# Instruction order of five engines from a list scheduler, other loads and masks for the first blocks, and a finer first FFN group, in a fused attention and FFN kernel

## The chip, the core and the metric

The kernel runs on one core of one Trainium2 chip. The metric is the device time of one execution in microseconds (us). Ratios between kernels are the mean time of one kernel's fast runs over the mean time of the other's fast runs of the same rounds on the same chip, so they are not quite the ratios of the medians that are quoted beside them.

## The reference

Sliding-window attention with four sink keys, then an RMS norm and a gated FFN. Batch, heads, sequence and head size are 4, 8, 768 and 64; the window is 128; the FFN takes 3072 tokens from 512 to 1536 and back.

```python
# (cut and condensed: scale, pos and rel are as usual)
def _attn_ref(q, k, v, n_sink, window):
    scores = scale * np.matmul(q, k.transpose(0, 1, 3, 2))
    keep = (pos[None, :] < n_sink) | ((rel >= 0) & (rel < window))
    scores = np.where(keep, scores, -1e9)
    a = np.exp(scores - np.max(scores, axis=-1, keepdims=True))
    a = a / (np.sum(a, axis=-1, keepdims=True) + 1e-09)
    return np.matmul(a, v)

def _moe_ref(x, w_gate, w_val, w_out, rms_g):
    xn = x / np.sqrt(np.mean(x * x, axis=-1, keepdims=True) + 1e-06) * rms_g
    g = xn @ w_gate
    return (g * (1.0 / (1.0 + np.exp(-g))) * (xn @ w_val)) @ w_out
```

The 3072 tokens are 24 blocks of 128, six blocks to a batch. Four blocks form an FFN group, so there are six groups, 0 to 5.

## The kernel before

A block goes through these steps: load q, k, v (the software DMA queue casts fp32 to bf16); transpose q and k (on PE up to block 11, by DMA from block 12 on); scores on PE; exp on ACT; mask on DVE (on POOL from block 12, but for the first block of a batch); AV on PE; normalise on DVE; square on ACT; six small RMS steps and the scaling `xr` on DVE; transpose `xr`; then the FFN of its group. Once in a batch the first four keys are copied into a sink tile, `ksk`, on DVE.

```python
    X_DMA_FROM = 8
    QK_DMA_FROM = 12                       # q, k of later blocks are transposed by DMA
    MANUAL = {mybir.EngineType.PE, mybir.EngineType.SP}
    # ... pools ...
    ring = ctx.enter_context(               # 8 PSUM banks, used in turn
        tc.tile_pool(name="ring", bufs=8, space=bass.MemoryType.PSUM))
    # ...
    load_q(0); load_k(0); load_q(1); load_v(0)   # (cut) all on the software queue
    # ...
    def unit_sink(b):
        ks = sink.tile([P, HP * KSW], BF16, name="ksk")
        nc.vector.memset(ks, 0.0)
        # ...
            nc.vector.tensor_copy(          # reads the transposed k of the batch's first block
                out=ksv[pr, :, hi * NS:(hi + 1) * NS], in_=QKT[b][pr, 1, :, 0:NS])
    # ...
        def gate():
            st["pg"] = slot("pg")
            mms(st["pg"], wg, G, fts, cols)
            # ... th = tanh(pg / 2) on ACT
        def val():
            pvl = slot("pvl")
            mms(pvl, wv, G, fts, cols)
            # ... p1 = (th + 1) * pg ; hT = p1 * pvl, both on DVE; they free the banks
    # ...
    with tc.manual_schedule(engines=MANUAL):
        # units of attention are woven by hand between the parts of the FFN
        for ft in range(0, FTN, 2):        # group 0 in two halves of two blocks
            fa += parts_f(0, (ft, ft + 1), slice(0, GN // 2))
            fb += parts_f(0, (ft, ft + 1), slice(GN // 2, GN))
        # ...
```

`MANUAL` names the engines that follow the written order. DVE, ACT and POOL are not among them: the framework's own scheduler orders these.

The softmax here doesn't subtract the row's maximum and nothing guards it: scores larger than these inputs give would overflow.

## Time and profile before

| | before |
|---|---|
| median of 3 runs | 270.05 us (269.97 to 270.92) |
| span of the profiled run | 269.7 us, granted clock 0.994 |
| first scores / first FFN matmul (PE timeline) | 10.33 / 23.22 us |
| first gate matmul of group 1 | 91.57 us |
| last matmul of the last projection starts | 265.49 us |

The first gate matmul of group 1 is the useful place to cut the run in two. The prediction took it from the chain of waits, where the step begins at 91.74; the PE timeline has the instruction at 91.57. The two cuts differ by 0.17 us and nothing hangs on that.

The page's line of engines (busy us, share of the span, instructions), and after it the first line of its chain of work that ended last:

```profile
PE 240.3 (89%) x1698; PEld 128.5 (48%) x1698; DVE 179.0 (66%) x471; ACT 135.5 (50%) x267; POOL 96.9 (36%) x128
```

The chain, as shares of the span by engine:

```profile
PE 80%; DVE 7%; ACT 6%; DMA 4%; issue 1%; POOL 0%; ACTq 0%; POOLq 0%
```

The windows view gives the busy time of each engine in a stretch, the granted clock, a DMA share (not used here) and the GB/s moved. Cut at the two marks of the table:

```profile
core 0: us, PE busy (x) PEld busy (x) DVE busy (x) ACT busy (x) POOL busy (x), PEclk, DMA share, GB/s
0.00:91.57 91.57, 66.26 (x634) 46.01 (x635) 60.09 (x184) 53.49 (x104) 70.74 (x90) 0.98 1.99 157
91.57:265.49 173.92, 173.92 (x1066) 82.51 (x1063) 118.96 (x288) 81.41 (x163) 26.20 (x38) 1.00 0.35 65
265.49:269.70 4.21, 0.16 (x1) 0.00 (x0) 0.00 (x0) 0.60 (x1) 0.00 (x0) 1.00 0.16 62
```

The middle row is a wall: PE is busy in all of its 173.92 us. The top row is where time can be won: PE is idle there for 91.57 - 66.26 = 25.3 us. The view of waits says what PE stood for before group 1 (total, times, longest):

```profile
PE pT L303 <- ACT qkT L237: 6.7, 5, 4.2
PE pqk L218 <- DMA qs<-in_q_dram: 4.8, 1, 4.8
PE pv L361 <- DVE et L325: 3.1, 5, 0.9
PE pxt L423 <- DVE y L384: 2.7, 1, 2.7
PE pxt L423 <- DVE xr L404: 2.1, 2, 1.1
```

The longest of the first line, 4.2 us, has ACT as its releaser, but ACT is not its cause. The chain in order of time leads further back, to a DMA transpose of block 12, four blocks ahead of the work in hand:

```profile
70.07 0.53 ACT qkT L237
70.59 7.69 DMA qkT<-ks
...
80.69 0.91 ACT qkT L237
```

And the timeline of DVE, then that of PE, shows how it got into the chain (start, duration, line, operation; in brackets the wait ahead of it and what ended it):

```profile
78.31 0.35 DVE L256 COPY ksk<-qkT 64x16 bf16<-64x16 bf16 x2 [3.64 <-DMA qkT<-ks]
78.69 0.18 DVE L368 RECIPROCAL rden<-pv 128x4 f32<-128x4 f32 x1
```

```profile
81.64 0.61 PE L303 MATMUL pT<-qkT 64*128 64x256 bf16 x8 [4.23 <-ACT qkT L237]
```

The framework had put the sink copy of batch 2 early in DVE's order. DVE stood there for 3.64 us until the transpose landed. The normalising of two AV results, whose matmuls had ended by 75.3 us, lay behind it, then squares on ACT, then the copy that the next scores need. The Trainium skill, "TensorE: Matmul & The Clock Gate", Part 1 (in the note on the array's architecture), says that ACT and DVE queues are strictly first in, first out; this trace agrees, with 3.64 us spent in front of work whose inputs were there.

The same page says the array runs at half clock until some 3.4 us of sustained work and again after an idle window as long. This trace agrees on the half rate: eight 128x256 gate matmuls take 1.87 us at 23 us and 0.87 from 31 us on, and after the 4.23 us gap 512-column matmuls start 0.427 us apart, and 0.216 again from 86 us.

### The profile page before, as it was taken

The page shows a single profiled execution, that of the slowest core. Times are in us where ns is not written, and L with a number is a line of the kernel's source. Part 1 is how long each engine was busy: PE and PEld are TensorE (multiplying, and loading weights), DVE is VectorE, ACT ScalarE, POOL GpSimd, SP SyncE. Part 2 cuts the span into 40 slices and gives each one's busy share as a digit, 9 for nine tenths or more (in the row PEclk, how much of TensorE's full clock was granted, in tenths as well). Part 3 has the DMA queues.
Part 4 walks back from the last instruction along what each step waited for, and adds up shares of the span by engine and source line. Part 5 has one row for each costly group of instructions (what it writes and reads, how often), then busy time and mean ns, then how long its engine had stood idle before and what let it go on. Part 6 is the DMA issues. An engine that isn't in the chain of part 4 may idle for free.

```text
span 269.7 us, 4662 instructions
## 1 busy us (share of the span) xinstructions
PE 240.3 (89%) x1698; PEld 128.5 (48%) x1698; DVE 179.0 (66%) x471; ACT 135.5 (50%) x267; POOL 96.9 (36%) x128
## 2 busy tenths in 40 slices
PE   1746997997748899999999999999999999999993
PEld 0324685784425444444454444445444544444441
DVE  2573499798736699982699845998528893087700
ACT  2453576677726664555566445664554531333311
POOL 8987477489968510043043200412430100000000
PEclk9999999999997999999999999999999999999999
DMA  8999999999999999217322054121231111210022
GB/s 55 135 159 193 199 156 193 175 156 149 162 145 177 159 177 100 58 29 168 79 58 43 19 133 129 31 45 19 60 100 39 21 22 39 78 39 2 0 78 78
DMA packets 105912, 25.99 MB, mean 96 GB/s; under 512 B 97185, under 2 KB 102817, under 8 KB 105890
## 3 DMA queue, kind: packets, MB, share of 16 engines
q0 software_dynamic: 80672, 14.16, 70.2%
q1 hardware_dynamic: 25218, 11.54, 19.7%
q8 instruction: 13, 0.21, 0.3%
q14 instruction: 9, 0.07, 0.1%
HBM read 28.31 MB, written 6.29 MB: 128 GB/s over the span
## 4 chain that ended last, share of the span: by engine, by line
PE 80%; DVE 7%; ACT 6%; DMA 4%; issue 1%; POOL 0%; ACTq 0%; POOLq 0%
PE pg L438 22%; PE pvl L438 22%; PE po L482 21%; PE pT L303 5%; DMA qkT<-ks 3%; PE pv L361 2%; PE pqk L218 2%; DVE et L325 2%; ACT qkT L237 2%; DMA ks<-in_k_dram 2%; PE pv L356 2%; PE pv L345 1%; DVE x L369 1%; PE pss L279 1%; ACT et L312 1%
## 5 line engine op out<-in xcount | busy, mean ns | idle before, releaser
L438 PE MATMUL pg<-xnt,wg 128*128 128x512 bf16 (+1 forms) x336 | 74.9, 352 | 1.3 <-ACT xnt L427 1.3
L438 PE MATMUL pvl<-xnt,wv 128*128 128x512 bf16 (+1 forms) x336 | 74.9, 352 | 0.0
L451 ACT ACTIVATE th<-pg 128x512 bf16<-128x512 f32 x72 | 43.3, 601 | 54.5 <-PE pg L438 54.2
L459 DVE SCALAR_TENSOR_TENSOR p<-th,pg 128x512 bf16<-128x512 bf16 x72 | 49.1, 682 | 32.3 <-ACT th L451 31.8
L482 PE MATMUL po<-wo,hT 128*128 128x512 bf16 x288 | 67.0, 383 | 0.0
L312 ACT ACTIVATE et<-pT 128x512 bf16<-128x512 f32 (+1 forms) x96 | 46.4, 568 | 13.1 <-PE pT L303 13.0
L467 DVE TENSOR_TENSOR hT<-p,pvl 128x512 bf16<-128x512 bf16 x72 | 49.3, 685 | 3.4
L327 POOL TENSOR_SCALAR_AFFINE_SELECT et<-et 128x512 bf16<-128x512 bf16 x20 | 14.5, 730 | 91.4 <-ACT et L312 83.0
L438 PEld LDWEIGHTS <-wv 128*128 128x128 bf16 x336 | 32.4, 99 | 28.8 <-issue 1.0
L438 PEld LDWEIGHTS <-wg 128*128 128x128 bf16 x336 | 32.2, 99 | 29.2 <-issue 2.3
L482 PEld LDWEIGHTS <-hT 128*128 128x128 bf16 x288 | 27.2, 99 | 30.8 <-issue 2.0
L488 ACT ACTIVATE osb<-po 128x512 f32<-128x512 f32 x24 | 14.4, 601 | 30.9 <-PE po L482 26.9
L98 POOL DMA_DIRECT2D ks<-in_k_dram x24 | 21.3, 888 | 8.5 <-DMA wo<-in_moe_w_out_dram 2.9
L98 POOL DMA_DIRECT2D qs<-in_q_dram x24 | 21.5, 894 | 7.2 <-DMA wo<-in_moe_w_out_dram 2.1
L325 DVE TENSOR_TENSOR et<-et,masks 128x1024 bf16<-128x1024 bf16 (+1 forms) x28 | 18.0, 651 | 8.5 <-ACT et L312 8.3
L376 ACT ACTIVATE sq<-x 128x512 bf16<-128x512 bf16 x24 | 15.1, 628 | 16.4 <-DVE x L369 16.4
L303 PE MATMUL pT<-qkT 64*128 64x256 bf16 (+1 forms) x192 | 15.4, 279 | 8.5 <-ACT qkT L237 6.7
L111 POOL DMA_DIRECT2D v<-in_v_dram x24 | 21.3, 888 | 4.4 <-DMA qs<-in_q_dram 1.4
L369 DVE TENSOR_TENSOR x<-pv,rden 128x256 bf16<-128x256 f32 x48 | 19.8, 420 | 0.6
L361 PE MATMUL pv<-v,et 128*128 128x65 bf16 x192 | 17.3, 200 | 3.1 <-DVE et L325 3.1
L404 DVE SCALAR_TENSOR_TENSOR xr<-x,r,gb 128x512 bf16<-128x512 bf16 x24 | 19.1, 798 | 0.6
L303 PEld LDWEIGHTS <-qkT 64*128 64x128 bf16 x192 | 7.9, 96 | 17.9 <-issue 17.2
(57 smaller groups left out, 178.5 us busy)
## 6 DMA issues: line engine op xcount, KB each, us to landing
out_dram<-osb SPq DMA_DIRECT2D x24, 256.0 KB, 2.0
qs<-in_q_dram POOLq DMA_DIRECT2D x24, 128.0 KB, 7.6
ks<-in_k_dram POOLq DMA_DIRECT2D x24, 128.0 KB, 7.4
v<-in_v_dram POOLq DMA_DIRECT2D x24, 128.0 KB, 8.2
wg<-in_moe_w_gate_dram POOLq DMA_DIRECT2D x4, 384.0 KB, 9.9
wv<-in_moe_w_val_dram POOLq DMA_DIRECT2D x4, 384.0 KB, 10.5
wo<-in_moe_w_out_dram POOLq DMA_DIRECT2D x2, 768.0 KB, 10.4
xnt<-xr SPq DMA_TRANSPOSE x16, 2.5
```

The costliest lines, as they stand in the source:

```text
L98: nc.gpsimd.dma_start(out=tl, in_=src[b, :, t * P:(t + 1) * P, :].rearrange("h t d -> t h d"),)
L111: nc.gpsimd.dma_start(out=V16[b][:, t, :, 0:D], in_=v[b, :, t * P:(t + 1) * P, :].rearrange("h t d -> t h d"),)
L303: nc.tensor.matmul(out=pT[(u, hi)][:, j * 256:j * 256 + w], lhsT=QKT[b][pr, 1, hp, t * P:(t + 1) * P], rhs=QKT[b][pr, 0, hp, t * P:t * P + w],
L312: nc.scalar.activation(out=et[:, 2 * hi:2 * hi + 2, 0:nq, :].rearrange("p x n c -> p x (n c)"), in_=pT[(u, hi)].rearrange("p (j c) -> p j ...
L325: nc.vector.tensor_tensor(out=ev, in0=ev, in1=mv, op=ALU.mult)
L361: nc.tensor.matmul(out=dest, lhsT=E[(g, u)][:, x, 0, :], rhs=V16[b][:, t, h, :], start=(t == 0), stop=True, skip_group_check=True,)
L369: nc.vector.tensor_tensor(out=x16[:, 4 * u:4 * u + 4, :], in0=pvv[:, :, 0:D], in1=rden.unsqueeze(2).to_broadcast((P, 4, D)), op=ALU.mult,)
L438: nc.tensor.matmul(out=ps[:, i * n:(i + 1) * n], lhsT=w_sb[:, kt, ft * P:(ft + 1) * P], rhs=XNT[G][:, kt, cols], start=(kt == 0), stop=(kt ...
L451: nc.scalar.activation(out=st["th"], in_=st["pg"], func=ACT.Tanh, scale=0.5,)
L459: nc.vector.scalar_tensor_tensor(out=p1, in0=st["th"], scalar=1.0, in1=st["pg"], op0=ALU.add, op1=ALU.mult,)
L467: nc.vector.tensor_tensor(out=HT[key][:, i:i + n, cols], in0=p1.rearrange("p (n c) -> p n c", n=n), in1=pvl.rearrange("p (n c) -> p n c", ...
L482: nc.tensor.matmul(out=st["po"], lhsT=HT[(G, ft // 2)][:, ft % 2, tb * P:(tb + 1) * P], rhs=wo[:, ft, :], start=(ft == 0), stop=(ft == FTN ...
```

## The change

The intent: let a small list scheduler inside the kernel decide the order on all engines, instead of a hand-made weave on PE and SP and the framework's order on the rest; and make the first blocks come sooner.

1. Every step becomes an operation of a plan, with a duration, its needs, a priority and the PSUM banks it takes and frees. A simulation in the kernel takes, again and again, the operation that can start earliest. Its order is then issued as the written order of all engines. Each bank is assigned by the plan.
2. q and k of blocks 0 and 1 are loaded as fp32 by the hardware queues of SP and ACT and cast on DVE.
3. Masks of blocks 0 and 1 are added on PE: -30000 by a matmul into the score banks, four of 512 columns for each block.
4. FFN group 0 runs block by block (128-wide matmuls, four columns of tiles at a time).
5. The weights come in other chunks and earlier than block 4; some PSUM copies may go to DVE or ACT, as the plan finds best.

```diff
-    MANUAL = {mybir.EngineType.PE, mybir.EngineType.SP}
+class Plan:
+    HOP = {"PE": 40, "ACT": 35, "DVE": 35, "POOL": 90, "SP": 60}
+    def run(self):
+        while left:
+            for e, found in cand.items():
+                for o in found:                       # earliest start wins, then priority
+                    ready = o["ready"] + self.HOP[e] if o["ready"] else 0
+                    if k:                             # k PSUM banks needed
+                        ready = max(ready, sorted(self.banks.values())[k - 1] + 40)
+                    key = (max(free[e], ready), o["prio"], ready, o["at"])
 ... (cut)
+    F32_LOADS = 2
+    PE_MASKS = 2
 ... (cut)
+    for g in range(F32_LOADS):
+        sp(370, 1300, lambda g=g: load_f32("q", q, g, nc.sync), (), [("qst", g)], -90 + g, work=900)
+        op({"ACT": (100, 1300, lambda g=g: load_f32("k", k, g, nc.scalar))}, ...)
+        for n in "qk":
+            dve(335, lambda n=n, g=g: cast(n, g), [(n + "st", g)], [(n, g)], -9 + g)
 ... (cut)
+            pe((240, 480, 590)[min(t, 2)], lambda g=g, u=u: av(g, u), ...)
+            dve(430, lambda g=g, u=u: normal(g, u), ...)
+        dve(1650, lambda g=g: rms(g), ...)            # seven instructions, one operation
+                sp(1250, 1700, lambda n=n, g=g: dma_t(n, g), ...)   # DMA transposes of q, k
 ... (cut)
+            for tb in range(GB):                      # group 0, block by block
+                for i in range(FTN // 4):
+                    ffn(G, 3 * tb + i, range(4 * i, 4 * i + 4), slice(tb * P, (tb + 1) * P), ...)
 ... (cut)
-    with tc.manual_schedule(engines=MANUAL):
+    order = plan.run()
+    with tc.manual_schedule():
+        for *_, fn, o in order:
+            if fn is not None:
+                fn()
```

The numbers in the calls are the plan's durations in nanoseconds.

## The prediction

> **What bounds it now.** The chain of waits is 80% PE. From group 1's first gate matmul (91.74 us) to the last projection (265.67), the windows view shows PE busy 173.91 of 173.93 us: pure matmul at its fast rate (four 128x512 take 0.86 us). The tail (eviction, store) is 4.03 us. All slack lies in the first 91.74 us: PE busy 66.4, idle 25.3. That work at its later rate would take about 52 us, an estimate from durations in the trace: FFN group 0 20.8, its projection 10.4, scores and AV of blocks 0 to 8 9, transposes 7, the rest 4. So some 14 us of "busy" is slow clock: eight 128x256 gate matmuls take 1.87 us at 23 us, 0.87 later. The Trainium skill, "TensorE: Matmul & The Clock Gate", Part 1, says the array runs at half clock until about 3.4 us of sustained work, and again after an idle window as long; the trace agrees: after a 4.23 us gap ending at 81.64, AV matmuls take 0.06 us each instead of 0.03. That gap: DVE, in order, stood 3.64 us at a sink copy waiting for a DMA transpose that took 7.7 us beside saturated loads; AV, squares and the copy for the next scores lay behind it.
>
> **What the change does.** PE work stays nearly equal: group 0's columns in 128-wide instead of 256-wide matmuls, plus eight 128x512 mask matmuls (1.7 to 3.4 us, early, while PE has slack). DVE loses four masks (0.69 each), gains four casts (about 0.4) and some transpose copies from ACT. By group 1's start DVE still has about 60 us of work (60.3 before): FFN 16, RMS 14, normalising 10, masks 9, the rest copies, sinks, constants. So DVE, at 85 to 90% use, sets the length of the early stage afterwards, not PE.
>
> Hardware queues without issue on POOL (1.01 and 0.88 us each) bring the first scores from 10.3 to about 7 us and the first FFN matmul from 23.2 to about 16; group 0 begins with one block instead of two. Weights move ahead of block 4. The Trainium skill, "DMA: Bandwidth & Descriptors", "Issuing engines are not separate DMA queues", says other queues save only issue time, so supply does not grow: block 7 lands near 45 us, ahead of need. Ordering all engines by expected readiness removes most early stalls and the 4.2 us gap.
>
> **Sum.** First gate of group 1 at about 73 us instead of 91.7 (about 8 us from the first 31 us, 10 from the rest). After that PE stays dense: 174 us (DVE needs only 119 of it, ACT 81); tail 4. Predicted 251.5 us, 8 in 10 between 246.5 and 259. Chances: faster by over 2% 0.93, within 2% 0.06, slower 0.01.
>
> **What would show it.** Right: PE idle before group 1 under 18 us; DVE over 80% busy from 15 to 70 us; PE busy in total 225 to 233 (240.3 before); first group-1 gate to last projection within 2 us of 174; tail within 0.5 of 4.03. Wrong: PE idle of some us after group 1's start, led by "DVE hT" or DMA transposes.
>
> **What would make it wrong.** Fixed orders on strict queues: where planned durations are too low (0.60 for FFN's DVE steps, 0.68 in the trace), one late operation holds ready ones behind it. DMA transposes, planned at 1.7 us, may take 7 while loads saturate the engines; PE would then wait in groups 1 and 2. Weights for group 0 landing later than 17 to 28 us would leave PE idle early, and slow again.

## More of the kernel before

The windows view gives a granted clock (PEclk) of 0.50 from 82.3 to 85.7 us. It gives 1.00 from 20 to 25 us, where the matmuls plainly run at half rate: for the first stretch of a run, go by the spacing of matmuls.

## The result, and the profile after

The changed kernel took 257.44 us in the median of four runs (256.51 to 257.9), beside 270.01 for the kernel before. The ratio is 0.9534, with a 95% interval of 0.9486 to 0.9583. The profiled run had a span of 256.2 us at a granted clock of 0.998.

| | before | after | predicted |
|---|---|---|---|
| time | 270.01 | 257.44 | 251.5 (246.5 to 259) |
| first scores | 10.33 | 10.71 | about 7 |
| first FFN matmul | 23.22 | 21.03 | about 16 |
| first gate matmul of group 1 | 91.57 | 71.01 | about 73 |
| from there to the last matmul of the last projection | 173.92 | 181.23 | 174 |
| PE busy, whole run | 240.3 | 238.7 | 225 to 233 |

The page's line of engines after the change, and the first line of its chain:

```profile
PE 238.7 (93%) x1880; PEld 130.8 (51%) x1906; DVE 183.6 (72%) x481; ACT 130.7 (51%) x273; POOL 93.1 (36%) x128
```

```profile
PE 66%; DVE 21%; ACT 5%; issue 3%; DMA 2%; ACTq 0%; DVEq 0%
```

PE shows 1880 matmuls against 1906 weight loads: 26 records of matmuls are missing from this trace. They leave holes in the records, but each hole is short, as the modelled ends of matmuls overlap. Windows after, cut at the same two marks, and the stretch from 15 to 70 us, for DVE (first before, then after):

```profile
core 0: us, PE busy (x) PEld busy (x) DVE busy (x) ACT busy (x) POOL busy (x), PEclk, DMA share, GB/s
0.00:71.01 71.01, 62.79 (x796) 46.42 (x801) 55.81 (x165) 45.44 (x99) 53.42 (x72) 1.00 1.95 171
71.01:252.24 181.23, 175.76 (x1087) 84.35 (x1106) 127.83 (x317) 84.64 (x173) 39.70 (x56) 1.00 0.58 77
252.24:256.20 3.96, 0.17 (x1) 0.00 (x0) 0.00 (x0) 0.60 (x1) 0.00 (x0) 0.90 0.33 127
```

```profile
15.00:70.00 55.00, 43.87 (x467) 33.87 (x465) 43.02 (x127) 34.27 (x69) 40.00 (x47) 1.00 2.02 173
```

```profile
15.00:70.00 55.00, 51.92 (x730) 41.18 (x731) 47.70 (x139) 39.51 (x87) 39.40 (x46) 1.00 2.07 175
```

Group 1 begins 20.6 us sooner. PE's idle time ahead of it fell from 25.3 to 71.01 - 62.79 = 8.2 us, so 17.1 of the 20.6 us are idle time and only 3.5 are busy time. Then 7.3 us are lost: the second stretch is longer by 7.3 us, of which 175.76 - 173.92 = 1.8 us is work (two more blocks of scores and some AV lie behind the cut) and 181.23 - 175.76 = 5.5 us is idle. PE's waits in that second stretch, where the kernel before had none:

```profile
PE g L737 <- DVE p L750: 2.7, 4, 0.8
PE g L737 <- ACT e L452: 0.8, 1, 0.8
PE av L503 <- DVE e L469: 0.5, 1, 0.5
PE o L770 <- issue: 0.2, 1, 0.2
```

A gate matmul waits for `p`. It does not read `p`: computing `p` (the SiLU product) is what frees the PSUM bank that the gate matmul will write. Scores hold four of the eight banks at such a moment. Here is one of the four, first DVE, then ACT, then PE, of the same timeline:

```profile
75.58 0.15 DVE L530 TENSOR_SCALAR m<-ms 128x1 f32<-128x1 f32 x1
...
76.66 0.75 DVE L547 SCALAR_TENSOR_TENSOR xr<-x,r,gb 128x512 bf16<-128x512 bf16 x1
77.33 1.28 DVE L750 SCALAR_TENSOR_TENSOR p<-th,g 128x512 bf16<-128x512 bf16 x2
```

```profile
74.94 1.06 ACT L744 ACTIVATE th<-g 128x512 bf16<-128x512 f32 x2
```

```profile
76.63 0.61 PE L439 MATMUL s<-qkT 64*128 64x256 bf16 x8
78.06 0.81 PE L737 MATMUL g<-xnt,wg 128*128 128x512 bf16 x3 [0.82 <-DVE p L750]
```

The seven RMS instructions, one operation of the plan, run unbroken from 75.58; `p` comes only then, although its input `th` was there by 76.00, and PE stands. (The two `p` take 1.28 us together, and the next instruction starts 1.19 us after the first: 0.60 us each. The mean of 0.68 that the page lists is a single one's busy time, which overlaps its successor's. The plan's 0.60 is right, and the prediction's remark that it is too low was a misreading.)

A running sum of PE's work shows when the gain was made. Each matmul is counted with the spacing that it has in the dense stage (512 columns 0.216 us, 256 0.109, 128 0.055, 65 0.029, 260 0.111; half of it where only 64 rows are used); it is worked out from the traces' PE records:

| PE work done by | 31 us | 60 us | 71 us | 91.7 us |
|---|---|---|---|---|
| before | 7.3 | 32.4 | 39.8 | 51.8 |
| after | 16.0 | 41.9 | 50.8 | 68.5 |
| lead | 8.7 | 9.5 | 11.0 | 16.7 |

Of the lead, 1.7 us are the mask matmuls, which the kernel before does not have. So the gain came in two pieces, about 7 us by 31 us and about 7 us between 60 and 92 us, where the kernel before has its wait at the sink copy. (The change's column is a little low, as some of its records are missing.)

### The profile page after: what moved, and what is told of

Same layout as the page of the kernel before. It is cut to its first block, busy times and chain, and to the rows that moved or that the text cites. A ratio compares the mean times of both kernels' runs of the same rounds, so it can differ in the third digit from the quotient of the medians.

```text
span 256.2 us, 5083 instructions
## 1 busy us (share of the span) xinstructions
PE 238.7 (93%) x1880; PEld 130.8 (51%) x1906; DVE 183.6 (72%) x481; ACT 130.7 (51%) x273; POOL 93.1 (36%) x128
## 4 chain that ended last, share of the span: by engine, by line
PE 66%; DVE 21%; ACT 5%; issue 3%; DMA 2%; ACTq 0%; DVEq 0%
PE o L770 21%; PE g L737 19%; PE v L737 17%; DVE xr L547 4%; DVE p L750 3%; DVE r L543 3%; DVE hT L760 3%; DVE x L515 3%; ACT e L452 2%; PE s L439 2%; DMA stage<-in_k_dram 2%; PE av L503 2%; DVE e L469 2%; PE av L498 1%; ACT sq L523 1%
## 5 line engine op out<-in xcount | busy, mean ns | idle before, releaser
L737 PE MATMUL g<-xnt,wg 128*128 128x512 bf16 (+1 forms) x427 | 69.4, 307 | 3.7 <-DVE p L750 2.7
L737 PE MATMUL v<-xnt,wv 128*128 128x512 bf16 (+1 forms) x422 | 70.6, 306 | 0.6
L750 DVE SCALAR_TENSOR_TENSOR p<-th,g 128x512 bf16<-128x512 bf16 x72 | 48.0, 683 | 28.5 <-ACT th L744 28.5
L770 PE MATMUL o<-wo,hT 128*128 128x512 bf16 x278 | 65.6, 379 | 0.7 <-issue 0.3
L744 ACT ACTIVATE th<-g 128x512 bf16<-128x512 f32 x72 | 42.5, 599 | 34.2 <-PE g L737 31.9
L452 ACT ACTIVATE e<-s 128x512 bf16<-128x512 f32 (+1 forms) x100 | 47.2, 556 | 13.6 <-PE s L439 13.5
L760 DVE TENSOR_TENSOR hT<-p,v 128x512 bf16<-128x512 bf16 x72 | 47.8, 682 | 1.9 <-PE v L737 1.3
L474 POOL TENSOR_SCALAR_AFFINE_SELECT e<-e 128x512 bf16<-128x512 bf16 x20 | 12.6, 634 | 87.5 <-ACT e L452 60.5
L312 POOL DMA_DIRECT2D q<-in_q_dram x22 | 19.6, 891 | 7.4 <-DMA wo<-in_moe_w_out_dram 2.6
L515 DVE TENSOR_TENSOR x<-av,rden 128x256 bf16<-128x256 f32 x48 | 20.4, 425 | 1.7
L503 PE MATMUL av<-v,e 128*128 128x65 bf16 x192 | 17.4, 197 | 1.1 <-DVE e L469 0.8
L498 PE MATMUL av<-v,e 128*128 128x65 bf16 x160 | 15.5, 195 | 0.0
```

What stands on the lines that cost most here:

```text
L312: nc.gpsimd.dma_start(out=T[name, g], in_=block_of(src, g))
L452: nc.scalar.activation(out=T["e", g, u][:, 2 * hi:2 * hi + 2, n0:n1, :].rearrange("p x n c -> p x (n c)"), in_=ps.rearrange("p (j c) -> p ...
L503: nc.tensor.matmul(out=dest, lhsT=T["e", g, u][:, x, 0, :], rhs=V16[b][:, t, h, :], start=(t == 0), stop=True, skip_group_check=True,)
L515: nc.vector.tensor_tensor(out=T["x16", g][:, 4 * u:4 * u + 4, :], in0=pvv[:, :, 0:D], in1=rden.unsqueeze(2).to_broadcast((P, 4, D)), op=AL ...
L737: nc.tensor.matmul(out=ps[:, i * n:(i + 1) * n], lhsT=w_sb[:, kt, ft * P:(ft + 1) * P], rhs=T["xnt", G][:, kt, cols], start=(kt == 0), sto ...
L744: nc.scalar.activation(out=T["th", key], in_=BANK[("g", key)], func=ACT.Tanh, scale=0.5,)
```

## The experiments

Twelve kernels ran. First, parts of the change were undone one at a time; then the wait at the sink copy was taken away in several kernels; then the stalls of the late stage were attacked. In the tables, "group 1" is the time of its first gate matmul and "late" is the time from there to the start of the last matmul of the last projection, both from the profiled run. Where an expectation names a time in us, the ratio times 270.0 is compared with it, as the kernel before ran between 270.0 and 272.0 us beside these runs.

### First loads by the software queue (a_sw_loads)

```diff
-    F32_LOADS = 2
+    F32_LOADS = 0
-    for g in range(F32_LOADS):
-        sw_block(g, "v")
+    for g in range(2):
+        sw_block(g, "v" if g < F32_LOADS else "qkv")
-               + ([("qp", g - 1)] if g else []), [("mb", g)], pa, takes=slots)
+               + ([("qp", g)] if g else []), [("mb", g)], pa, takes=slots)
```

(The last edit keeps the plan from giving all eight banks to masks before block 1 is transposed.)

> The changed kernel, but q and k of blocks 0 and 1 come as bf16 from the software queue, ahead of v and the weights, as in the kernel before (no fp32 staging, no casts). Theory (the early start is worth something): first scores and first FFN matmul come 2 to 3 us later and the time rises from 257.4 to 259.5 to 261. Rival (supply after the first blocks and DVE set the early stage, the queue of the first loads does not): 256.5 to 258.5, and the first gate matmul of group 1 stays within 1 us of 71.0.

Measured: 259.69 us, ratio 0.9558 (0.9524 to 0.9592); group 1 at 72.38, late 181.2. The loss is 0.2% against the change's 0.9534, within the noise. By the ratio (258.1 us at a base of 270.0) the rival's range holds; the plain median lies in the theory's, as the kernel before was slower beside it too (271.97). Group 1 comes 1.4 us later, a little outside the rival's 1 us. But the theory's reason fails: the first scores come earlier without the hardware queues, at 8.63 us instead of 10.71, and the first FFN matmul too (20.59, 21.03). So the hardware queues for the first two blocks are worth nothing that can be measured in the time. The timeline of DVE in the changed kernel shows why:

```profile
6.89 0.43 DVE L308 CAST k<-stage 128x512 bf16<-128x512 f32 x1 [2.17 <-DMA stage<-in_k_dram]
7.24 0.86 DVE L308 CAST q<-stage 128x512 bf16<-128x512 f32 x1
```

The first line is k of block 1. q of block 0 had landed at 5.40 us, but its cast stood behind a cast for which DVE waited 2.17 us. The fixed order was made for a landing that did not happen so. No kernel with these two casts exchanged was run.

### Masks of the first blocks on DVE (a_dve_masks)

```diff
-    PE_MASKS = 2
+    PE_MASKS = 0
```

> The changed kernel, but blocks 0 and 1 are masked on DVE like the rest (no eight mask matmuls). Theory (DVE sets the length of the early stage, so its four masks of 0.69 us count): 258.5 to 260.5. Rival (PE has slack to spare and DVE as well while the first loads land): within 0.8 us of 257.4.

Measured: 263.4 us, ratio 0.969 (0.9645 to 0.9735); group 1 at 77.39, late 180.8. The loss is larger than the theory allowed for four masks of 0.69 us, so neither text fits. The timeline of DVE in this kernel names another cause:

```profile
71.37 0.49 DVE L582 COPY ksk<-qkT 64x16 bf16<-64x16 bf16 x2 [4.41 <-DMA qkT<-k]
```

The plan, with slightly other operations, had put the sink copy of batch 2 earlier among DVE's work, and DVE stood there till the DMA transpose of block 12 landed at 71.28 us. PE then had a gap of 5.4 us. That is the wait of the kernel before once more.

### Group 0 in halves (a_halves)

```diff
-            for tb in range(GB):
-                for i in range(FTN // 4):
-                    ffn(G, 3 * tb + i, range(4 * i, 4 * i + 4), slice(tb * P, (tb + 1) * P), ...)
+            for h in range(2):
+                for i in range(FTN // 2):
+                    ffn(G, 6 * h + i, range(2 * i, 2 * i + 2), slice(2 * h * P, 2 * (h + 1) * P), ...)
-                        and (G or key[2] == tb * P)]
+                        and (G or key[2] == tb // 2 * 2 * P)]
```

> The changed kernel, but FFN group 0 runs in halves of two blocks (256-wide matmuls) as before, not block by block. Theory (starting FFN on one block fills PE and DVE earlier): first FFN matmul moves from 21.0 to about 24 us and the time rises by 2 to 4 us, to 259.5 to 261.5. Rival (DVE work and the landing of weights set the stage, the width does not): within 1 us of 257.4.

Measured: 262.34 us, ratio 0.9659 (0.9613 to 0.9704), so 1.25% of 270 or 3.4 us slower than the change; first FFN matmul at 23.75 us, group 1 at 77.52. The theory holds by the ratio (260.8 us at a base of 270.0; the plain median is 0.8 us above its range). Part of the loss may again be the sink copy, which waits 1.7 us here. But by 60 us, before that copy, this kernel had done 37.4 us of PE work against 41.9: block by block had gained 4.5 us by then.

### The framework's order on DVE, ACT and POOL (a_auto_order)

```diff
-    with tc.manual_schedule():
+    with tc.manual_schedule(engines={mybir.EngineType.PE, mybir.EngineType.SP}):
```

> The changed kernel with its order kept on PE and SP only; ACT, DVE and POOL are ordered by the framework's own scheduler, as in the kernel before. Theory (most of the gain is the order on DVE and ACT): it gives back at least 6 of the 12.6 us, 263.5 or more, with DVE waiting some us on a DMA transpose or a projection out of turn. Rival (the order of PE and of the loads, the new bank choice and block-by-block FFN make the gain): 256 to 260.

Measured: 278.3 us, ratio 1.0244 (1.021 to 1.0278); group 1 at 91.30. That is slower than the kernel before: more than the whole gain is gone. Lines from the timelines of DVE and of PE:

```profile
71.69 0.48 DVE L582 COPY ksk<-qkT 64x16 bf16<-64x16 bf16 x2 [12.90 <-DMA qkT<-k]
```

```profile
74.67 0.61 PE L562 MATMUL x<-ident,xr 128*128 128x128 bf16 x4 [14.15 <-DVE xr L547]
```

The same sink copy, now for 12.9 us.

Two kernels and the kernel before now showed one wait, 3.6 to 12.9 us long; it is 1.7 us in a_halves, and in the change itself it is there too, with 0.86 us:

```profile
72.71 0.35 DVE L582 COPY ksk<-qkT 64x16 bf16<-64x16 bf16 x2 [0.86 <-DMA qkT<-k]
```

The next runs take its cause away: block 12 is transposed on PE, so that the sink copy no longer depends on a DMA transpose.

### The kernel before without that wait (b_pe_t13)

```diff
-    QK_DMA_FROM = 12
+    QK_DMA_FROM = 13
```

> The kernel before, but q and k of block 12 are transposed on PE instead of by DMA, so that the sink copy for batch 2, early in the order of DVE, no longer waits for a DMA transpose (3.64 us in its trace, then AV matmuls at 0.06 us instead of 0.03). Theory (this one wait and the slow clock after it are a large part of what the change gained): PE loses no stretch of over 2 us after 25 us, and the time falls by 5 to 8 us, to 262 to 265 at a base of 270. Rival (the wait hides others behind it; loads and DVE hold the stage up as long): less than 2 us.

Measured: 267.5 us, ratio 0.9874 (0.9783 to 0.9965); group 1 at 87.48, late 174.4. The wait and the 4.2 us gap are gone and group 1 comes 4.1 us sooner; the time falls by 1.3%, or 3.4 us. This lies between the two texts; the interval, 0.9 to 5.9 us, reaches into both. The wait is real, but at the measured mean it is only about a quarter of the 12.6 us. By the running sum above, this kernel has done 4.0 us more of PE work than the kernel before at 91.7 us, so the wait, with the slow stretch behind it, makes 4.0 of the 7 us that the change gains between 60 and 92 us.

### The kernel before with its written order on all engines (b_manual_all)

```diff
-    with tc.manual_schedule(engines=MANUAL):
+    with tc.manual_schedule():
```

> The kernel before, but DVE, ACT and POOL also follow the order in which its program is written, with nothing else of the change. Theory (the gain comes from taking the sink copy of batch 2 out of DVE's early order, for which any order by hand will do): the 3.6 us wait is gone; as the written order is not tuned to DVE and ACT, some of that comes back as other waits; 263 to 269. Rival (a good order, found by the list scheduler, is what counts): 270 or more.

Measured: 295.6 us, ratio 1.0922 (1.0842 to 1.1002); group 1 at 103.31, late 186.7. The rival holds, by more than it said. DVE does not wait for the DMA transpose here, yet an order written with PE in mind makes waits everywhere else: PE's waits for ACT and DVE come to over 30 us. Fixing the order is no gain in itself; it has to be a good order.

### The framework's order without that wait (a_auto_t13)

The edit of a_auto_order, and block 12 on PE as in b_pe_t13.

> The changed kernel with DVE, ACT and POOL ordered by the framework (278.3 us, with a wait of 12.9 us for the DMA transpose of block 12 in DVE and a gap of 14.2 us in PE), but with block 12 transposed on PE. Theory (that one wait is nearly all of what the order of DVE, ACT and POOL is worth): 261 to 266. Rival (the order is worth more than this wait): above 268.

Measured: 264.26 us, ratio 0.9763 (0.9691 to 0.9834); group 1 at 77.92. The time lies in the theory's range: one misplaced copy of 0.5 us cost 13 to 14 us (278.3 to 264.3; the ratios 1.0244 and 0.9763 say 13.0). "Nearly all" says too much, as some 19 us lie between a_auto_order and the change. What is left between this kernel and the change, 0.9763 and 0.9534 or about 6 us, is what the plan's order on DVE, ACT and POOL is worth beyond that wait; the change with block 12 on PE, the exact partner, was not run. In this kernel PE starts at 8.8 us instead of 3.1, as the constant for the masks comes late in DVE's order. In a_auto_order, which starts at 8.0 us, PE is only 3.4 us behind the change at 60 us (38.5 of 41.9 us of work).

### DVE masks without that wait (a_dve_masks_t13)

The edit of a_dve_masks, and block 12 on PE.

> The changed kernel with DVE masks for blocks 0 and 1 (4.2 us slower than the change, with a wait of 4.4 us for the DMA transpose of block 12), but with block 12 transposed on PE. Theory (the masks on PE themselves are worth nothing, the plan only happened to place the sink copy worse): the loss shrinks to under 1.5 us, ratio to the kernel before 0.952 to 0.959. Rival (masks on PE are worth their 4 us): ratio 0.965 or more.

Measured: 258.41 us, ratio 0.9552 (0.9484 to 0.9621); group 1 at 72.36, late 180.7. The theory holds. The masks on PE, as such, are worth nothing that can be measured; the 4 us of a_dve_masks were the sink copy. (The comparison is with the change, whose block 12 is transposed by DMA and whose own wait is 0.86 us.)

### The late stage: RMS in two operations (a_rms_split)

```diff
-        dve(1650, lambda g=g: rms(g),
-            [("ms", g), "gb"] + ..., [("xr", g)], early)
+        dve(1000, lambda g=g: rms(g), [("ms", g)] + ..., [("rr", g)], early)
+        dve(650, lambda g=g: rms_x(g), [("rr", g), "gb"] + ..., [("xr", g)], early)
```

> The changed kernel with the RMS chain of a block as two operations of the plan instead of one of 1.65 us (six small ones; then the scaling), so that FFN's DVE steps, which free PSUM banks, may go between. Theory A (the unbroken RMS chain holds up the freeing of banks): the late stage, from the first gate matmul of group 1 to the last projection, falls from 181.2 to 177 or less and the time by 3 us or more, ratio to the kernel before 0.944 or less. Theory B (the plan's durations are off: AV takes 0.59 us in it and 0.35 in the trace, normalising 0.43 and 0.55, so PE arrives before DVE has freed the bank): late stage stays over 179, ratio 0.949 to 0.957.

### The late stage: durations from the trace (a_costs)

```diff
-            pe((240, 480, 590)[min(t, 2)], lambda g=g, u=u: av(g, u), ...)
+            pe((125, 245, 360)[min(t, 2)], lambda g=g, u=u: av(g, u), ...)
-            dve(430, lambda g=g, u=u: normal(g, u), ...)
+            dve(555, lambda g=g, u=u: normal(g, u), ...)
-        dve(1650, lambda g=g: rms(g), ...)
+        dve(1750, lambda g=g: rms(g), ...)
 ... (scores, square and sink copies likewise)
```

> The changed kernel, plan unchanged in form, but with durations as the trace shows them: AV 0.125, 0.245, 0.36 us instead of 0.24, 0.48, 0.59; scores 0.35 instead of 0.57 beside the switch; normalising 0.555 instead of 0.43; RMS 1.75 instead of 1.65; square 0.63 instead of 0.72; sink copies a little longer. Theory B (durations off): stalls in the late stage fall from 6.5 to under 3 us, late stage 178 or less, ratio to the kernel before 0.935 to 0.945, unless the sink copy of batch 2 lands on a late DMA transpose. Theory A (the unbroken RMS chain): stalls stay over 5 us, ratio 0.950 to 0.957.

### Both (a_costs_split)

> Both: the trace's durations in the plan, and the RMS chain in two. If either alone takes the stalls away, this is no better than that one by more than 1 us; if both count, the late stage falls to about 176 (174 of the kernel before, and 2 of work that came later) and the ratio to 0.935 or less.

These three ran together, in five rounds. PE's idle time in the late stage was summed for each kernel over all spacings of matmuls more than 0.2 us longer than the dense spacing; by this count the changed kernel has 6.5 us, with short gaps between AV matmuls that the windows view does not show as idle. Such a count depends on how missing records are treated; the two columns of PE's idle time, from the windows view, do not.

| | ratio to before (95%) | group 1 | late | stalls in late | idle in late | idle before group 1 |
|---|---|---|---|---|---|---|
| change | 0.9534 (0.9486 to 0.9583) | 71.01 | 181.2 | 6.5 | 5.5 | 8.2 |
| a_rms_split | 0.9553 (0.9509 to 0.9597) | 73.56 | 179.7 | 1.8 | 1.8 | 11.3 |
| a_costs | 0.9618 (0.9573 to 0.9662) | 76.72 | 179.1 | 3.1 | 2.5 | 13.3 |
| a_costs_split | 0.9565 (0.9522 to 0.9608) | 75.38 | 177.1 | 1.6 | 1.6 | 13.0 |

By the numbers set beforehand, a_rms_split fell where theory B put it (late stage over 179, ratio within 0.949 to 0.957), and a_costs where neither text put it. The waits say more. Either remedy takes most stalls out of the late stage; the line of `g` waiting for `p` is gone from all three. It stands, at 1.8 to 2.8 us, in a_sw_loads, a_dve_masks, a_halves and a_dve_masks_t13, whose edits touch neither the RMS operation nor these durations; in a_dve_masks, for instance:

```profile
PE g L737 <- DVE p L750: 1.8, 3, 0.7
```

So each remedy does what it was meant to do. But group 1 begins 2.5 to 5.7 us later than in the change, and the total does not fall: PE's idle time before group 1 grew by 3.1 to 5.1 us. The stalls were moved ahead of the cut rather than removed. In all three DVE waits there for the transpose of block 12 (1.6, 0.5 and 0.7 us), and that led to the last run.

### One more true duration: the DMA transposes (a_costs_split_lat)

```diff
-                sp(1250, 1700, lambda n=n, g=g: dma_t(n, g), ...)
+                sp(1250, 8500 if g < 14 else 2500, lambda n=n, g=g: dma_t(n, g), ...)
```

> As the run with the trace's durations and the RMS chain in two, with one more number in the plan set as the trace shows it: the DMA transposes of blocks 12 and 13 land 8.5 us after issue (7 to 10 in every trace) instead of 1.7. Nothing else differs; the scheduler then places the sink copy of batch 2 behind the start of group 1 instead of ahead of it. Theory (the stalls that both remedies took out of the late stage came back ahead of group 1, because DVE there stands at the sink copy till the transpose lands at 71 to 73 us): no wait of DVE for the transpose, first gate matmul of group 1 at 70 to 72 us instead of 75.4, late stage still 178 or less, ratio to the kernel before 0.932 to 0.945. Rival (DVE and ACT simply have too much work there, wherever it is placed): first gate matmul at 74 us or later, or the late stage grows by what is saved; ratio 0.950 to 0.958.

Measured: 257.5 us, ratio 0.9518 (0.9489 to 0.9548); group 1 at 73.75, late 178.1. The plan moved the sink copy behind the start of group 1, and DVE waits for no transpose any more. The late stage is dense again, as the windows view of this kernel shows:

```profile
0.00:73.75 73.75, 61.77 (x808) 45.78 (x809) 56.03 (x168) 45.76 (x99) 56.15 (x75) 1.00 1.88 176
73.75:251.88 178.13, 177.89 (x1098) 84.32 (x1097) 125.74 (x315) 84.52 (x173) 38.42 (x54) 0.99 0.56 73
```

Yet the time is no better than the change's, within the noise; the two intervals overlap. Group 1 comes at 73.75, neither at 70 to 72 nor at 74 or later. The largest waits of PE in this kernel:

```profile
PE s L421 <- DVE idnos L257: 3.1, 1, 3.1
PE av L503 <- DVE e L469: 3.1, 1, 3.1
PE x L564 <- DVE xr L549: 2.2, 3, 1.2
```

The second line is a new gap, at 69 us, and matmuls after it run at the slow clock, as PEclk (0.50) says:

```profile
74.10:77.50 3.40, 3.40 (x10) 1.22 (x8) 1.76 (x8) 1.76 (x4) 0.87 (x1) 0.50 1.60 155
```

The profiles of the three kernels of the table have such a stretch of 3.4 to 6.8 us near the cut too (PEclk 0.50 from 74.7, 73.2 and 73.3 us); the change's has none. What it costs was not separated.

Block 7 is the last one that group 1 needs. Its scores run at 60.1 us in the change and at 64.1 in this kernel; from there to the first gate matmul are 10.9 and 9.6 us, mostly exp, mask, normalising, RMS and copies one after the other. With group 0 done, PE has nothing else to do. So of the theory, the part about the sink copy and the late stage holds, and the part about the total does not; the ratio is the rival's, but its reason, too much work, is not shown: DVE itself idles 1.16 us in that stretch, waiting for ACT. The later start of block 7 is the plan's own doing: run by itself, the plan puts these scores at 56.8 us in the change and at 61.0 in this kernel. Why it does so when it is given truer durations was not settled.

No kernel of this study is clearly faster than the change.

## Why the prediction was right or wrong

**The time.** 257.44 us lies inside 246.5 to 259, and "faster by over 2%" was right. The sum was off by 5.9 us from its centre. By its terms: first gate of group 1 at 71.0 instead of 73 (2 us better); the stage after that 181.2 instead of 174 (7.2 us worse); the tail 3.96 instead of 4 (the rest is rounding and the difference between a profiled span and the median). That the total fell inside the range is in part luck: one term came out better and one worse, and, as follows, one had the wrong cause.

**The step that failed: "After that PE stays dense: 174 us (DVE needs only 119 of it, ACT 81)."** It measured 181.2. 1.8 us are work that the cut no longer has ahead of it. 5.5 us are PE idle, which the kernel before has not. The argument "DVE needs only 119 of 174 us" is about averages; a bank is freed by one particular DVE instruction at one particular time. The stalls went with either of two remedies, splitting the unbroken RMS operation or giving the plan true durations (6.5 to 1.8 or 3.1 us), and the waits for `p` stayed in the kernels that had neither, so both have a part in them. The text had named "PE idle of some us after group 1's start, led by DVE hT or DMA transposes" as the sign of its being wrong; the sign came, led by `p`, not `hT`.

**"DVE, at 85 to 90% use, sets the length of the early stage."** DVE was busy 47.70 of 55 us between 15 and 70 us, 87% (78% before). Under 18 us of PE idle were expected before group 1; 8.2 were measured. That DVE's amount of work is the limit was not shown, though: four masks less or more made no difference (0.9552 and 0.9534), and the last run had DVE waiting at the critical point.

**"About 8 us from the first 31 us."** The lead was 8.7 us of PE work at 31 us (7 without the masks). The size came out right by luck, as its cause was wrong. The prediction gave it to the hardware queues, with first scores at 7 us; they came at 10.71 (and the first FFN matmul at 21.03, not 16), and without the hardware queues the time is the same (0.9558). Running group 0 block by block (2.4 us of lead at 31 us, 4.5 at 60) and the plan's order on DVE and ACT (3.5 us at 31 us, by a_auto_order's 12.5 of 16.0) are what the runs show. The rest of that lead, which may come from weights that land at 10.3 instead of 18.2 us for the first chunk (256 instead of 384 KB), was not tried alone.

**"10 from the rest", with the 4.2 us gap.** The gap is shown: b_pe_t13 takes it out of the kernel before and gains 1.3% (0.4 to 2.2), group 1 coming 4.1 us sooner. What made the rest of the 7 us gained between 60 and 92 us was not singled out. In the change the same wait is there with 0.86 us. It is chance where the plan puts this copy: neighbours of the change waited 1.7 and 4.4 us, and the framework's order 12.9. The plan's call says 1.7 us for the transposes of block 12, and with the plan's model of the queues they come to 3.7 and 3.8 us; they took 8.5 and 9.2 us in the change.

**"Some 14 us of busy is slow clock", PE busy 225 to 233 in total.** It was 238.7. Ahead of group 1 PE is busy for 62.8 us with 50.8 us of work; the difference of 12.0 was 14.6 before. In the first 25 us, where PE works in short bursts at the slow clock, it is 8.3 us (6.8 before): the four mask matmuls of 512 columns at 3 us take 1.89 us together, 0.43 apart, instead of 0.216. The gain was idle time above all (17.1 us) and clock very little.

**"Supply does not grow."** Right in the main. In the first 15 us it did grow, to 164 GB/s from 108 in a_sw_loads; some 35 of these are only the double width of fp32 (an estimate: four loads of 256 instead of 128 KB). Later it evened out. The last chunk of gate and value weights landed at 30.7 instead of 35.3 us, and the last load of block 7 at 49.4 instead of 44.3: things changed places. All weights and blocks 0 to 7 together had landed by 49.4 us, and by 51.3 before. The Trainium skill, "DMA: Bandwidth & Descriptors", section "Issuing engines are not separate DMA queues", says that issuing from several engines saves only the time of issuing; with k of block 0 landing at 4.00 instead of 6.47 us, q of block 0 at 5.40 instead of 4.80, and no gain in the time, these runs agree.

## What to carry to other kernels

On a queue that keeps its order, one small instruction placed ahead of its input's arrival can hold up everything behind it: look for the instruction with the longest wait before it, ask which far-off transfer it waits for, and give the scheduler that transfer's time under load, not its time when alone (here that took the wait away, though the total did not fall beyond the noise). A fixed order that depends on planned times moves such an instruction about with every edit, so a part that looks costly when undone (masks, 4 us) may only have moved it; repeat the test with the wait taken away before believing the number. And when a stage is called dense because its busiest engine has work for all of it, check also that what frees the buffers comes in time: stalls can be removed there and come back ahead of it.

## What the Trainium skill lacked or had wrong

- "DMA: Bandwidth & Descriptors", "DMA Transpose (X-bar)": the page gives a bandwidth for a transpose, but not how long one takes beside saturated loads. Here a 128x512 bf16 transpose within SBUF landed 2.4 to 2.5 us after issue in the median once the loads were done (after 110 us), and 7 to 10 us after it between 60 and 80 us, while the loads filled the queues; loads of q, k and v issued between 60 and 70 us in the change took 6.4 to 12.2 us.
- No page that was looked up tells what a single early instruction costs on a strictly ordered engine queue. "TensorE: Matmul & The Clock Gate", Part 1, says that DVE and ACT queues are strict; here one copy pair of 0.5 us at the wrong place made a wait of 12.9 us on DVE, a gap of 14.2 us on PE, and 13 to 14 us of the time.
- "TensorEngine Tiling (Array Packing)", "Key Properties", says that a change of tiling mode drains the array and gives no size. Here, in the dense stage, the 64-row score matmuls start in pairs, 0.106 us from pair to pair at 256 columns; a 512-column matmul that follows starts 0.20 us after the last pair, and the first score matmul starts 0.312 us after the 512-column matmul ahead of it instead of 0.216: about 0.10 us for each change.
